# Attention and two expert layers on one core: three sets of weights for piece 0 alone become one, and the layer operands get a pool of their own

## The chip, the cores and the metric

One core of one Trainium2 chip runs the whole kernel in one launch. The metric is device time in microseconds. Three runs of the kernel before took 894.58, 894.58 and 893.46 us, median 894.58. A further execution was profiled: 893.12 us, of which the profile's span, from the first to the last instruction, is 891.3. The core's TensorE ran at a mean granted clock of 0.993 of its full speed in it. Durations below come from this one execution.

## The reference

Queries, keys and values have 4 batches, 8 heads, 576 positions and 64 channels. Attention stays inside chunks of 64 positions. Its output, as 2304 tokens x 512 channels, goes through two layers with different weights (512 x 2048 and 2048 x 512 each).

```python
scores = scale * np.matmul(q_c, k_c.transpose(0, 1, 2, 4, 3))     # chunks of 64
scores = scores - np.max(scores, axis=-1, keepdims=True)
attn = np.exp(scores)
attn = attn / (np.sum(attn, axis=-1, keepdims=True) + 1e-09)
out = np.matmul(attn, v_c)
...
h = x @ w_in1;  g = h * np.clip(h + 3.0, 0.0, 6.0) / 6.0;  x = g @ w_out1
h = x @ w_in2;  g = np.maximum(h, 0.0) + np.log1p(np.exp(-np.abs(h)));  out = g @ w_out2
```

The layers' weights arrive as 64-bit numbers and are turned into float32 on the chip.

## The kernel before

**Pieces and steps.** The 2304 tokens are cut into five pieces: piece 0 has 256 tokens, pieces 1 to 4 have 512. The 2048 hidden channels are cut into 16 sets of 128; a set of weights is one 512 x 128 block of `w_in` (half 0) and one 128 x 512 block of `w_out` (half 1). A *step* (`Step`, line 565) is one layer, one piece and one set. Every operand of a product is held as a high and a low part (fp32r), and a product takes three of the four combinations. So a step has a first product of 12 matmuls into one PSUM bank `h` (`first_product`, line 626: eight with `wh`, four with `wl`; the weights are the stationary operand and the piece's `x` is the moving one), an activation on ScalarE, VectorE and GpSimd that ends in `gh` and `gl` (`activate`, line 651), and a second product of 12 matmuls that adds into the output banks (`second_product`, line 736). In layer 1 the second product moves `gh`/`gl` over the weights, in layer 2 it moves the weights. PE gets the first product of step i+2 ahead of the second product of step i.

**Weights.** `convert` (line 281) loads the raw 64-bit words of half a set into a staging tile (512 KB a half) and makes float32 of them: two ScalarE passes (lines 299 and 302), three VectorE passes (a clamp on line 305, a shift on 311, the sign on 316) and an addition on GpSimd (line 322). The result stays in a tile of its own, `w0_0` to `w15_1`. Each time a piece begins a set, `split` (line 334) makes `wh` on ScalarE and `wl` on GpSimd or VectorE from it. The raw words of layer 1 are staged in tiles that later hold x of pieces 2 to 4 (`RAW`, line 869).

**Attention.** A `Unit` (line 372) is 512 columns of scores: two units for piece 0, four for each other piece. Its work on PE is a transpose of q and k (pieces 0 and 1 by matmul, lines 420 and 427; the others on VectorE, line 400), scores (line 466), a transpose of p (line 474) and the weighing with v (line 517). Between these stand five to eight passes on VectorE and some on ScalarE. It ends by filling the piece's `x<piece>_0` (high) and `x<piece>_1` (low). v arrives by halves of a piece in the tiles `v`, of which there are two (`load_v`, line 357).

**Order.** No order is written out by hand. All work is put into a list of jobs with their engines, costs, tiles and due times. `Schedule.run` (line 58 on) plays them through, takes for each engine the job that is due first among those that can start, and gives each a tile as soon as its former user is done. The instructions are issued in this order, so each engine, and the one DMA queue (SP), works strictly in it; an instruction that waits holds up all behind it on its engine. Due times come from a timetable of the steps (line 598): it begins at 15 us and adds each step's PE time. The units of pieces 2 to 4 are spread over the time of the piece before (line 879).

**The steps around the change.** `JOIN` is 3: with sets 0, 1 and 2 only piece 0 is worked on; from set 3 on each set serves piece 1 and then piece 0; after set 15 piece 1 does sets 0, 1 and 2 alone. Then come pieces 2, 3 and 4 of layer 1, pieces 1, 2 and 3 of layer 2, and at last pieces 4 and 0 of layer 2 side by side. In the joint stage piece 0's output takes the banks H1 and A1, so `h` has one bank, H0.

**Places in SBUF.** All tiles but the identity come from one pool, `sb`. A tile is placed when the program first uses it, behind the ones placed before: the tiles that also stage q, k and raw words (x2, x3, x4) lie low in each partition, between 17,024 and 101,184 bytes; `wh0` and `wl0` lie between 101,568 and 115,904, piece 0's x from 115,904 to 124,096, `gh` and `gl` between 134,336 and 152,768, x1 at 154,816 and 177,344, `wh1` and `wl1` between 165,056 and 175,296.

Of the kernel before, what the change touches and what calls it, by code (L numbers as in the profile page):

```python
# [8 lines left out]
F32 = mybir.dt.float32  # L9
# [161 lines left out]
def kernel(  # L171
# [20 lines left out]
    NT, DM = out.shape  # L192
    DFF = w_in1.shape[1] // 2
    P = 128
    CH = 64
    KD = DM // P
    KF = DFF // P
    NP = H // 2
# [8 lines left out]
    NPC = len(pieces)  # L207
    assert sum(tokens) == NT and tokens == [HALF] + [512] * (NPC - 1)

    const = ctx.enter_context(tc.tile_pool(name="const", bufs=1))  # L210
    sb = ctx.enter_context(tc.tile_pool(name="sb", bufs=1))
    psum = ctx.enter_context(tc.tile_pool(name="psum", bufs=1, space=bass.MemoryType.PSUM))

    BANKS = ("y0", "y1", "y2", "y3", "H0", "H1", "A0", "A1")
    bufs = dict.fromkeys(BANKS, 1)
    for f in range(KF):
        bufs[f"w{f}_0"] = bufs[f"w{f}_1"] = 1
    for x in range(NPC):
        bufs[f"x{x}_0"] = bufs[f"x{x}_1"] = 1
    bufs.update(  # L220
        wh0=2, wh1=2, wl0=2, wl1=2, gh=3, gl=3, cg=3, v=2, raw=2, qkT=1, p=3, ps=2, r=3, m=3, sm=3, rs=3,
    )
    sch = Schedule(bufs)
    ident = const.tile([P, P], F32, name="ident")

    def runs(x, a, n):

        done, at = 0, 0
        for b, s, m in pieces[x]:
            lo, hi = max(a, at), min(a + n, at + m)  # L230
            if lo < hi:
                yield lo - a, hi - lo, b, s + lo - at
            at += m
# [17 lines left out]
    def sp(n_bytes, rate):  # L251
        return {"SP": (n_bytes / rate, "dma")}
# [103 lines left out]

    def load_v(x, c, deps=(), due=1e9):

        t = Buf("v", [P, 2, DM], F32, "v")
        for g in range(2):  # L360
            for off, m, b, s in runs(x, (2 * c + g) * P, P):
                def load(e, off=off, m=m, b=b, s=s, g=g):
                    nc.sync.dma_start(
                        out=t.tile[off:off + m, g, :].rearrange("p (h d) -> p h d", h=H),
                        in_=v[b, :, s:s + m, :].rearrange("h p d -> p h d"),
                    )
                v_load.setdefault((x, 2 * c + g), []).append(sch.job(load, sp(m * DM * 4, 218e3), deps, (t,)))
            v_buf[x, 2 * c + g] = t
# [199 lines left out]
        def __init__(self, layer, x, f, first, last):  # L568
            self.layer, self.x, self.f, self.n, self.first, self.last = layer, x, f, tokens[x], first, last

    JOIN = 3
    seen = {}
    steps = []

    def add_step(layer, x, f):
        n = seen[layer, x] = seen.get((layer, x), 0) + 1
        steps.append(Step(layer, x, f, n == 1, n == KF))


    for f in range(KF):  # L580
        if f >= JOIN:
            add_step(1, 1, f)
        add_step(1, 0, f)
    for f in range(JOIN):
        add_step(1, 1, f)
    for x in range(2, NPC):
        for f in range(KF):
            add_step(1, x, f)
# [6 lines left out]
    NS = len(steps)  # L595


    t = 15.0
    for i, s in enumerate(steps):
        s.at = t  # L600
        t += 24 * (s.n / 2400.0 + 0.0133) + (2.0 if i < JOIN else 0.0) + (0.3 if s.layer == 1 else 0.0)

    def when(layer, x, nth=0):
        return [s.at for s in steps if (s.layer, s.x) == (layer, x)][nth]
# [241 lines left out]
    for u in range(2):  # L846
# [4 lines left out]
            for y, src in enumerate((q, k))  # L851
        ])
    load_v(0, 0)
    for un in units:
        un.attend()
    join = when(1, 1)
    for u in range(NP):
# [4 lines left out]
            for y, src in enumerate((q, k))  # L862
        ])
    load_v(1, 0)
    load_v(1, 1)
    for un in units[2:]:
        un.attend()

    RAW = ["x3_1", "x4_0", "x4_1", "x2_0", "x3_0", "x2_1"]
    for f in range(KF):  # L870
        tag = RAW[f] if f < len(RAW) else ("x3_1", "x4_0", "x4_1", "x3_0")[(f - len(RAW)) % 4]
        raw = Buf(tag, [P, 2, 1024], I32, "raww")
# [3 lines left out]
    before = [j for un in units for j in un.turned]  # L876
    for x in range(2, NPC):
        a, b = when(1, x - 1), when(1, x)
        us = [Unit(x, (u,), a + (b - a) * (u + 1) / NP - 2.0, ("A0", "A1"), x > 2) for u in range(NP)]
        for un in us:  # L880
            un.load(before)
            before = un.loads
        for c in range(2):
            load_v(x, c, [l for g in range(2 * c) for l in v_load[x, g]] or v_load[x - 1, 3])
        for un in us:
            un.attend()
# [17 lines left out]
    with tc.manual_schedule():  # L904
        nc.scalar.preload_act_table_set("natural_log_exp_and_others")
        for j in sch.run():
            for b in j.uses:
                if b.tile is None:
                    pool_ = psum if b.tag in BANKS else sb
                    b.tile = pool_.tile(b.shape, b.dt, tag=b.tag, name=b.name, bufs=bufs[b.tag])  # L910
            j.fn(j.engine)

# [30 lines left out]
```

## Time and profile before

| | |
|---|---|
| median of three runs | 894.58 us |
| profiled execution | 893.12 us |
| span of its profile | 891.3 us |
| PE busy | 867.3 us, 97% |
| VectorE busy | 608.8 us, 68% |
| ScalarE busy | 545.6 us, 61% |
| GpSimd busy | 456.1 us, 51% |

PE is the engine of the matmuls, DVE is VectorE, ACT ScalarE, POOL GpSimd, and SPq the queue that issues DMAs. A line L636 is line 636 of the kernel. Matmuls overlap in the pipeline, so the time of one is read from the start of one group to the start of the next, not from its duration. The releaser behind an arrow is what ended a wait.

### The profile page before, as it was taken

How to read it: one execution, taken by the hardware profiler on the slowest of the kernel's cores; microseconds unless marked ns; L12 is line 12 of the kernel's file. 1: busy time of each engine (PE TensorE's matmuls, PEld its weight loads, DVE VectorE, ACT ScalarE, POOL GpSimd, SP SyncE). 2: the span in 40 equal slices, each digit the busy share in tenths (PEclk: the TensorE clock that was granted, in tenths of full speed). 3: DMA queues.
4: the chain of work that ended last, by engine and by line, in shares of the span. 5: the costliest groups of instructions: out<-in, count | busy, mean ns of one | idle time of the engine just before them, and what ended most of it. 6: DMA issues, size and time to landing. Idle time of an engine off the chain costs nothing.

```text
span 891.3 us, 13771 instructions
## 1 busy us (share of the span) xinstructions
PE 867.3 (97%) x5112; PEld 711.5 (80%) x5112; DVE 608.8 (68%) x935; ACT 545.6 (61%) x987; POOL 456.1 (51%) x359
## 2 busy tenths in 40 slices
PE   7889999999999999999999999999999999999996
PEld 5777888887778778788888888888888888887875
DVE  5989999845345546479887655655565557778775
ACT  5855565455444545478777666666666666565654
POOL 1545556543444444469987444444444444555551
PEclk9989999999999999999999999999999999999999
DMA  9991531240112210046640000100010001000002
GB/s 275 247 236 56 158 111 56 41 79 1 25 25 48 46 28 25 24 142 192 200 151 1 1 1 0 48 1 1 0 48 1 1 0 48 1 1 1 1 1 71
DMA packets 101571, 53.33 MB, mean 60 GB/s; under 512 B 76672, under 2 KB 95104, under 8 KB 101504
## 3 DMA queue, kind: packets, MB, share of 16 engines
q1 hardware_dynamic: 101504, 52.45, 21.8%
q8 instruction: 40, 0.66, 0.3%
q14 instruction: 27, 0.22, 0.1%
HBM read 47.71 MB, written 4.72 MB: 59 GB/s over the span
## 4 chain that ended last, share of the span: by engine, by line
PE 73%; DVE 13%; ACT 5%; POOL 3%; DMA 2%; issue 2%; SPq 1%; DVEq 0%; POOLq 0%; ACTq 0%
PE y L762 33%; PE h L636 24%; PE h L643 12%; DVE r L708 3%; POOL wl L265 2%; POOL gl L265 1%; PE z L762 1%; DVE l L704 1%; DVE cg L316 1%; DVE cg L305 1%; PE ss L466 1%; DVE cg L311 1%; DVE gl L265 1%; ACT r L693 1%; DVE r L714 1%
## 5 line engine op out<-in xcount | busy, mean ns | idle before, releaser
L265 POOL TENSOR_TENSOR wl<-w,wh 128x512 fp32r<-128x512 f32 x257 | 338.4, 1318 | 321.8 <-ACT wh L260 235.8
L636 PE MATMUL h<-x,wh 128*128 128x512 f32 (+1 forms) x1280 | 295.9, 373 | 1.9 <-DVE r L674 1.7
L636 PEld LDWEIGHTS h<-x,wh 128*128 128x128 f32 x1280 | 225.9, 189 | 48.6 <-DVE r L674 2.8
L260 ACT ACTIVATE wh<-w 128x512 fp32r<-128x512 f32 x262 | 164.9, 629 | 129.2 <-PE y L762 66.0
L643 PE MATMUL h<-x,wl 128*128 128x512 f32 (+1 forms) x640 | 162.0, 374 | 0.0
L643 PEld LDWEIGHTS h<-x,wl 128*128 128x128 f32 x640 | 112.8, 189 | 22.5
L322 POOL TENSOR_TENSOR w<-w,cg 128x512 int32<-128x512 int32 x64 | 86.7, 1361 | 63.0 <-DVE cg L316 46.8
L265 DVE TENSOR_TENSOR gl<-h,gh 128x512 fp32r<-128x512 f32 x96 | 66.2, 690 | 49.2 <-ACT gh L260 48.9
L699 DVE TENSOR_SCALAR d<-r 128x512 f32<-128x512 f32 x80 | 33.0, 413 | 80.8 <-ACT r L693 80.8
L260 ACT ACTIVATE gh<-h 128x512 fp32r<-128x512 f32 x96 | 57.3, 597 | 47.7 <-DVE h L719 32.2
L708 DVE SCALAR_TENSOR_TENSOR r<-l,r 128x512 f32<-128x512 f32 x80 | 77.5, 969 | 5.1 <-DVE l L704 0.5
L762 PE MATMUL y<-wh,gh 128*128 128x512 f32 x256 | 72.9, 397 | 1.2 <-ACT gh L260 1.1
L674 DVE SCALAR_TENSOR_TENSOR h<-r,h 128x512 f32<-128x512 f32 x48 | 33.3, 694 | 58.6 <-ACT r L667 58.6
L762 PE MATMUL y<-gh,wh 128*128 128x512 f32 x256 | 72.1, 395 | 0.0
L762 PE MATMUL y<-gh,wl 128*128 128x512 f32 x256 | 71.3, 393 | 0.0
L762 PE MATMUL y<-wl,gh 128*128 128x512 f32 x256 | 70.7, 390 | 0.0
L762 PE MATMUL y<-gl,wh 128*128 128x512 f32 x256 | 70.6, 390 | 0.0
L762 PE MATMUL y<-wh,gl 128*128 128x512 f32 x256 | 70.5, 389 | 0.0
L667 ACT ACTIVATE r<-h 128x512 f32<-128x512 f32 (+1 forms) x80 | 44.2, 552 | 37.4 <-PE h L643 37.3
L260 ACT ACTIVATE gh<-r 128x512 fp32r<-128x512 f32 (+1 forms) x64 | 33.3, 521 | 52.7 <-DVE r L719 24.2
L704 DVE TENSOR_TENSOR l<-l,d 128x512 f32<-128x512 f32 x80 | 54.2, 678 | 14.9 <-ACT l L696 13.1
L762 PEld LDWEIGHTS y<-wh,gh 128*128 128x128 f32 x256 | 47.3, 188 | 16.6 <-ACT gh L260 5.7
(77 smaller groups left out, 1142.5 us busy)
## 6 DMA issues: line engine op xcount, KB each, us to landing
raww<-in_moe_w_in_dram SPq DMA_DIRECT2D x32, 512.0 KB, 4.1
raww<-in_moe_w_out_dram SPq DMA_DIRECT2D x32, 512.0 KB, 4.7
v<-in_v_dram SPq DMA_DIRECT2D x16, 256.0 KB, 5.8
out_dram<-o SPq DMA_DIRECT2D x16, 256.0 KB, 2.0
raw<-in_q_dram SPq DMA_DIRECT2D x32, 64.0 KB, 2.5
raw<-in_k_dram SPq DMA_DIRECT2D x32, 64.0 KB, 2.5
nat<-in_q_dram SPq DMA_DIRECT2D x4, 256.0 KB, 6.5
nat<-in_k_dram SPq DMA_DIRECT2D x4, 256.0 KB, 6.7
```

The source lines that it names most:

```text
L260: nc.scalar.activation(out=out, in_=in_, func=AF.Copy)
L265: (nc.vector if e == "DVE" else nc.gpsimd).tensor_tensor(out=out, in0=in0, in1=in1, op=ALU.subtract)
L305: nc.vector.tensor_scalar(out=t.tile, in0=t.tile, scalar1=LEAST, scalar2=MOST, op0=ALU.max, op1=ALU.min)
L322: nc.gpsimd.tensor_tensor(out=w.tile, in0=w.tile, in1=g.tile.bitcast(I32), op=ALU.add)
L636: nc.tensor.matmul(out=h.tile[:, :n], lhsT=hi.tile[:, kk * P:(kk + 1) * P], rhs=x.tile[:, kk, :], start=(kk == 0 and m == 0), stop=False,)
L643: nc.tensor.matmul(out=h.tile[:, :n], lhsT=lo.tile[:, kk * P:(kk + 1) * P], rhs=xh.tile[:, kk, :], start=False, stop=(kk == KD - 1),)
L667: nc.scalar.activation(out=of(r), in_=of(h), func=AF.Relu, bias=3.0)
L674: lambda e: nc.vector.scalar_tensor_tensor(out=of(g), in0=of(r), scalar=6.0, in1=of(h), op0=ALU.min, op1=ALU.mult), dve(n), (j,), (h, r), due,
L699: lambda e: nc.vector.tensor_scalar(out=of(d), in0=of(r), scalar1=1.0, scalar2=1.0, op0=ALU.add, op1=ALU.subtract), dve2(n), (u,), (r, d),
L704: lambda e: nc.vector.tensor_tensor(out=of(l), in0=of(l), in1=of(d), op=ALU.subtract),
L708: lambda e: nc.vector.scalar_tensor_tensor(out=of(r), in0=of(l), scalar=0.0, in1=of(r), op0=ALU.min, op1=ALU.add), dve(n, not stays), (j,) ...
L762: nc.tensor.matmul(out=bank.tile[:, col:col + width], lhsT=lhs, rhs=rhs, start=(s.first and m == 0 and opens), stop=(s.last and m == 2 and ...
```

## The change

Three things. `JOIN` becomes 1, with another order: piece 0's set 0, then piece 1's set 0, then for sets 1 to 14 piece 1 before piece 0, and for set 15 piece 0 before piece 1; no set is left for piece 1 alone. The timetable begins at 28 us, and the four units of piece 2 are due in the second half of the joint stage (2/6 of it later). The second v tile of piece 1 is `x4_1`, and the first raw words go through the tiles in another order. And a pool `streamed`, opened behind `sb`, holds `wh`, `wl`, `gh`, `gl` and all x.

```diff
     sb = ctx.enter_context(tc.tile_pool(name="sb", bufs=1))
+    streamed = ctx.enter_context(tc.tile_pool(name="streamed", bufs=1))
...
+    STREAMED = {"wh0", "wl0", "wh1", "wl1", "gh", "gl"} | {f"x{x}_{part}" for x in range(NPC) for part in range(2)}
...
-        t = Buf("v", [P, 2, DM], F32, "v")
+        t = Buf("x4_1" if (x, c) == (1, 1) else "v", [P, 2, DM], F32, "v")
...
-    JOIN = 3
+    JOIN = 1
...
     for f in range(KF):
-        if f >= JOIN:
-            add_step(1, 1, f)
-        add_step(1, 0, f)
-    for f in range(JOIN):
-        add_step(1, 1, f)
+        for x in (1, 0) if JOIN <= f < KF - 1 else (0, 1):
+            add_step(1, x, f)
...
-    t = 15.0
+    t = 28.0
...
-    RAW = ["x3_1", "x4_0", "x4_1", "x2_0", "x3_0", "x2_1"]
+    RAW = ["x3_1", "x4_0", "x2_0", "x2_1", "x3_0", "x4_1"]
...
-        us = [Unit(x, (u,), a + (b - a) * (u + 1) / NP - 2.0, ("A0", "A1"), x > 2) for u in range(NP)]
+
+        late = 2 if x == 2 else 0
+        us = [
+            Unit(x, (u,), a + (b - a) * (u + 1 + late) / (NP + late) - 2.0, ("A0", "A1"), x > 2) for u in range(NP)
+        ]
...
-                    pool_ = psum if b.tag in BANKS else sb
+                    pool_ = psum if b.tag in BANKS else streamed if b.tag in STREAMED else sb
```

## Rows read from the trace of the kernel before

**Rows 1.** The page, busy time, share of the span and instructions of each engine.
```profile
PE 867.3 (97%) x5112; PEld 711.5 (80%) x5112; DVE 608.8 (68%) x935; ACT 545.6 (61%) x987; POOL 456.1 (51%) x359
```
**Rows 2.** Table by stage: length, busy us (instructions) by engine, clock, DMA share, GB/s.
```profile
44.76:69.61 24.85, 20.09 (x130) 17.06 (x128) 22.00 (x38) 13.51 (x27) 10.90 (x9) 0.86 0.88 213
69.61:174.57 104.96, 104.11 (x764) 89.72 (x764) 101.50 (x139) 59.85 (x116) 61.54 (x46) 1.00 0.31 86
...
387.85:476.28 88.43, 88.43 (x385) 72.03 (x384) 76.75 (x120) 70.74 (x126) 77.95 (x62) 1.00 0.52 157
493.30:564.02 70.72, 70.72 (x313) 58.56 (x312) 41.23 (x65) 46.70 (x78) 33.73 (x26) 1.00 0.00 1
564.02:652.66 88.64, 88.64 (x385) 71.95 (x384) 53.10 (x84) 58.79 (x97) 41.34 (x32) 1.00 0.03 13
751.01:784.39 33.38, 33.38 (x169) 28.25 (x168) 25.07 (x35) 19.72 (x40) 19.02 (x16) 1.00 0.09 32
784.39:870.73 86.34, 86.14 (x421) 69.91 (x420) 66.06 (x91) 50.42 (x101) 46.97 (x40) 1.00 0.00 1
```
**Rows 3.** What PE waited for, 0 to 100 us: total, times, longest.
```profile
PE z L762 <- ACT wh L260: 3.8, 1, 3.8
...
PE h L636 <- DVE r L674: 1.7, 2, 0.9
```
**Rows 4.** The same view, 100 to 891 us.
```profile
PE y L762 <- ACT gh L260: 1.1, 2, 0.9
```
**Rows 5.** PE in order of time: start, us, instruction, idle before.
```profile
44.76 2.02 PE L636 MATMUL h<-x,wh 128*128 128x512 f32 x8
...
51.44 1.22 PE L762 MATMUL z<-gh,wh 128*128 128x256 f32 x4 [3.76 <-ACT wh L260]
...
65.64 1.11 PE L636 MATMUL h<-x,wh 128*128 128x256 f32 x8
...
67.07 0.64 PE L762 MATMUL z<-gh,wh 128*128 128x256 f32 x4
...
69.61 0.73 PE L636 MATMUL h<-x,wh 128*128 128x512 f32 x2 [0.94 <-DVE r L674]
```
**Rows 6.** The same view, one step of pieces 1 and 2 in layer 2.
```profile
498.74 1.98 PE L636 MATMUL h<-x,wh 128*128 128x512 f32 x8
500.55 1.07 PE L643 MATMUL h<-x,wl 128*128 128x512 f32 x4
501.46 1.07 PE L762 MATMUL y<-wh,gh 128*128 128x512 f32 x4
...
602.80 2.03 PE L636 MATMUL h<-x,wh 128*128 128x512 f32 x8
604.67 1.09 PE L643 MATMUL h<-x,wl 128*128 128x512 f32 x4
605.60 1.08 PE L762 MATMUL y<-wh,gh 128*128 128x512 f32 x4
```
**Rows 7.** DVE by line, 9.3 to 45.8 us: count, busy us, mean ns, idle before.
```profile
L311 DVE TENSOR_SCALAR cg<-cg 128x512 int32<-128x512 int32 x6 | 3.5, 580 | 0.1
L316 DVE SCALAR_TENSOR_TENSOR cg<-raww,cg 128x512 int32<-128x512 int32 x5 | 3.4, 683 | 0.0
L305 DVE TENSOR_SCALAR cg<-cg 128x512 f32<-128x512 f32 x6 | 2.8, 459 | 0.3 <-ACT cg L299 0.3
...
L674 DVE SCALAR_TENSOR_TENSOR r<-r,h 128x256 f32<-128x256 f32 x3 | 1.2, 411 | 0.0
```
**Rows 8.** ACT in order of time, the wait behind which the split stood.
```profile
48.83 0.66 ACT L302 ACTIVATE w<-raww 128x512 int32<-128x512 uint32 x1 [3.85 <-DMA raww<-in_moe_w_in_dram]
```
**Rows 9.** The DMA queue in order of time.
```profile
43.30 0.42 SPq L291 DMA_DIRECT2D raww<-in_moe_w_in_dram  x1
```
**Rows 10.** PE in order of time, piece 2's last unit: scores, and past its weighing.
```profile
169.37 1.15 PE L466 MATMUL ss<-qkT 64*64 64x64 f32 x32
...
187.57 1.19 PE L643 MATMUL h<-x,wl 128*128 128x512 f32 x4
```

## The prediction

> **What bounds the kernel now.** I read the page's busy shares first, then a table by stage, then what TensorE (PE) waited for, then the order of PE's work in the first 70 us, and last the spacing of its matmuls inside a step. The shares say PE: 867.3 of 891.3 us [rows 1]. The waits say where it is not PE: before 100 us it waited 3.8 us once for a weight split and 1.7 us for VectorE (DVE) [rows 3], and after 100 us 1.1 us in all [rows 4]. So time can come only from the head, up to about 70 us, or from PE's own work running faster.
>
> *The head.* Piece 0 does its first three products alone; piece 1 enters at 44.76 us; the next second product comes at 51.44 after the 3.76 us wait; from 69.61 on PE hardly stops [rows 5]. [...] I need one number for the head: when PE would have started if it had done nothing but products, without a gap. By 69.61 it had done five first products of piece 0 (1.44 us each at full clock: the row at 65.64 and its wl products end 1.43 later at 67.07), four second products of piece 0 (1.44 each), two first and one second product of piece 1 (2.72 each): 9 x 1.44 + 3 x 2.72 = 21.1 us. One score product of piece 2 (1.1 us) was done too. So the effective start is 69.6 - 21.1 - 1.1 = 47.4 us.
>
> *The products.* The table by stage splits the dense part by piece. In layer 2, piece 1 takes 70.72 us for 13 steps (312 of the matmuls counted), 5.440 each; piece 2 takes 88.64 for 16, 5.540 each; in layer 1 piece 4 takes 88.43 for 16, 5.527 [rows 2]. It is the same work on the same shapes, and PE is busy 100% in all three. Inside a step the first product shows it: from the start of the eight wh matmuls to the start of the wl matmuls it takes 500.55 - 498.74 = 1.81 us for piece 1 and 604.67 - 602.80 = 1.87 for piece 2, and the four wl matmuls 0.91 and 0.93 [rows 6]. That is some 6.5 ns a matmul. The weights and the elementwise work are the same; what differs is where the moving operand lies. Tiles of a pool lie in the order of their first use, and adding up sizes gives their start in a partition: x2 and x3 at 17,024 to 53,888 bytes, x4 at 70,272 and 92,992, piece 0 at 115,904, gh at 134,336, x1 at 154,816 and 177,344. The slow moving operands are the low ones; gh and x1, above 134,336, run at 0.227 us a matmul.
>
> **The change, part by part.**
>
> *Layer operands in a pool of their own.* It removes no instruction. Pools are stacked in the order opened: const ends at 17,024, what stays in `sb` is 109,120 bytes, so `streamed` (102,400 bytes) begins at 126,144 and every x, gh, gl, wh, wl lies above. If the row reading holds, pieces 2 to 4 run as piece 1 does: in layer 1 pieces 2 and 3 (32 steps x 0.100; their windows hold attention too, so I take layer 2's difference) and piece 4 (16 x 0.087), in layer 2 pieces 2 and 3 (32 x 0.100): 3.2 + 1.4 + 3.2 = 7.8 us. The last stage, piece 4 beside piece 0, is different: four pairs take 33.38 us, 8.35 each, but the ten from 784.39 take 86.34, 8.63 each [rows 2]: there the elementwise chain sets the pace, and a faster product only waits longer. I count the other six pairs, 6 x 0.087 = 0.5. Sum 8.3 us. Upper bound, all sixteen: 9.2. Lower bound by place: the first tile of the pool, half of x2, lies at 126,144 to 134,336, below the lowest address shown fast with 512 columns; if it stays slow, 8 of 12 first-product matmuls in 32 steps do: 32 x 0.100 x 2/3 = 2.1 lost, 6.2 left. Lower bound by cause: 0, if place is not it.
>
> [...]
>
> *Piece 1 from the first set of weights on.* The matmuls are the same in number. Gone are re-splits of three sets at the end of the joint stage (six wh, six wl, on ScalarE and GpSimd, beside a PE that has no wait there), so nothing. What moves is the head. What sets when piece 1 is ready is DVE, which works almost without a gap until piece 1's fills are done (0.3 us is all the idle time before the groups shown [rows 7]); the first product of piece 1 starts at 44.76 [rows 5]. Up to there DVE runs 6 clamps (0.459 us), 6 shifts (0.580), 5 signs (0.683) of the weight conversion and 3 products of piece 0's activation (0.41) [rows 7]. Before piece 1 is needed the new order asks for three conversions (both halves of set 0, the first half of set 1) and one activation: out of the way go 3 x 0.459 + 3 x 0.580 + 2 x 0.683 + 2 x 0.41 = 5.3 us. Piece 1 starts at 44.76 - 5.3 = 39.5. The work put behind it comes due at once: five conversions (8.6 us) within the next 11 us, and the normal activations; here I expect waits.
>
> *Waits after the start.* Before, the 24.85 us from 44.76 to 69.61 held 2 x 2.72 + 2 x 1.44 + 3 x 1.44 + 2.72 + 1.1 = 16.5 us of work; 8.4 were lost to waits and the low clock. One cause was the ACT queue: its next instruction, a conversion of a set far ahead, waited 3.85 us for weights issued only at 43.30 behind piece 2's q and k loads [rows 8, 9], and the split that PE needed stood behind it. The change puts piece 2's units later (2/6 of the stage), so their loads come due later; a like mistake can still happen. Loss after the new start: at best the 1.7 us that DVE cost [rows 3], at worst 8.4 again; I take half of it, 4.2. New effective start: 39.5 - 1.44 (piece 0's first product, done before) + 4.2 = 42.3, against 47.4: 5.1 us gained. Bounds: 7.6 with 1.7 lost; 0.9 with 8.4; if piece 1 is no earlier than now, -0.2, and with 8.4 lost -4.4.
>
> *Other tiles for v and raw words.* The second v tile of piece 1 goes to x4_1, raw sets 2, 3 and 5 change tile. No copy or load more; a v load need not wait for piece 0's v. Set 2 now waits for x2_0, which piece 0's q leaves before 10 us; set 5 waits for piece 1's last weighing and is used 30 us later. I take 0; bounds -0.5 and +0.5, one 0.5 us issue slot either way.
>
> *Sum.* 8.3 + 5.1 = 13.4 us. The profiled execution took 893.12 us: 879.7. The median of the timed runs is 894.58, 1.46 above it: 881.2, say 881.
>
> **The rivals.**
> A, *place is nothing*: only the head gains. For it: the x2 to x4 steps differ from x1's in neighbours too. Against: the slow-down sits on the first product alone, and the step is as long in layer 1 (5.527) as in layer 2 (5.540), whose elementwise work differs [rows 2]. 894.6 - 5.1 = 889.5.
> [...]
> C, *piece 2 late*, slower than before: today three steps of piece 1 alone (3 x 5.44 us from 174.57 on), with no weights left to convert, precede piece 2 and let DVE finish its attention; they go, and its four units are pushed into the second half of the joint stage. The last unit, scores to weighing, takes 187.57 - 169.37 = 18.2 us [rows 10]. If it starts when piece 2 is due, PE waits 18.2: 894.6 - 13.4 + 18.2 = 899.4. It turns slower above a wait of 13.4. Against: the last unit's due time, 2 us before piece 2, is unchanged.
>
> **How the numbers follow.** Forecast 0.57, B 0.18, A 0.13, C 0.08, the rest 0.04. The range takes the forecast's bounds (9.2 + 7.6 gives 877.8; 3 us below for waits I do not see), A and B, and the upper end 891 is the placement gain with the worst head (890.7): 875 to 891. About 0.2% (1.8 us) is what a measurement tells from no change. Faster: forecast, B, A and half the rest: 0.88. Same 0.04, slower 0.08.
>
> **What would show it.** Place: steps of pieces 2 to 4 in layer 2 at 5.44 us; at 5.54, A. Half of x2: piece 2 alone near 5.50. Head: piece 1's first product near 40 us, PE dense well before 69 us; a first product at 45 or later refutes the DVE count. C: a PE gap where piece 2 begins in layer 1. The prediction is wrong if both groups of steps stay as they are or the joint stage ends later than 191 us.

## The result, and the profile after

The changed kernel takes 879.08 us (median of 4 runs, 877.49 to 880.32), the one before 894.02 beside it (4 runs, 893.23 to 894.58): ratio 0.9833, 95% interval 0.9814 to 0.9851. The forecast was 881. The profiled execution took 879.37 us with a span of 877.6, 13.7 less than before. Cut at the first products of piece 2 (layer 1), of layer 2 and of its last stage, the spans give:

| stretch | before, us | after, us | change | forecast |
|---|---|---|---|---|
| start to piece 2 of layer 1 | 191.35 | 184.75 | -6.6 | -5.1 |
| layer 1, pieces 2 to 4 | 284.93 | 282.20 | -2.7 | -4.6 |
| layer 2, piece 1 | 87.74 | 87.93 | +0.2 | 0 |
| layer 2, pieces 2 and 3 | 177.28 | 174.08 | -3.2 | -3.2 |
| last stage and end | 149.97 | 148.62 | -1.35 | -0.5 |

The page's first part and the table by stage of the changed kernel answer to [rows 1, 2]; the columns are the same.

```profile
PE 857.7 (98%) x5112; PEld 709.6 (81%) x5112; DVE 603.7 (69%) x934; ACT 540.6 (62%) x986; POOL 443.3 (51%) x349
```
```profile
35.52:68.80 33.28, 29.93 (x162) 24.08 (x157) 28.84 (x45) 21.48 (x43) 17.99 (x13) 1.00 0.66 162
68.80:174.79 105.99, 104.64 (x771) 89.73 (x770) 99.73 (x148) 62.79 (x123) 58.15 (x41) 1.00 0.37 100
...
379.91:466.95 87.04, 87.04 (x385) 72.07 (x384) 75.62 (x119) 68.56 (x125) 76.86 (x62) 1.00 0.52 159
484.17:554.89 70.72, 70.72 (x314) 58.56 (x312) 41.44 (x65) 46.69 (x78) 33.67 (x26) 1.00 0.00 1
554.89:641.93 87.04, 87.04 (x386) 72.07 (x384) 53.09 (x84) 57.81 (x97) 41.44 (x32) 1.00 0.04 13
738.59:771.63 33.04, 33.04 (x170) 28.27 (x168) 25.33 (x35) 20.34 (x41) 18.90 (x16) 1.00 0.09 33
```

All three product windows now run at 5.440 us a step: 70.72 / 13, and 87.04 / 16 where 88.64 and 88.43 stood. In the head the clock column reads 1.00 where it read 0.86; that is this one execution: the other three had mean granted clocks of 0.994 to 0.996, against 0.999 here, and took 877.49 to 880.32 us, so the clock is not what the gain hangs on. PE in order of time shows piece 1 starting at 35.52 instead of 44.76, and one step of piece 2 in layer 2 with 1.81 us for the eight wh matmuls, as piece 1 had [rows 5, 6]:

```profile
31.73 1.22 PE L636 MATMUL h<-x,wh 128*128 128x256 f32 x8
...
35.52 1.43 PE L636 MATMUL h<-x,wh 128*128 128x512 f32 x5
...
43.13 0.71 PE L762 MATMUL z<-gh,wh 128*128 128x256 f32 x4 [0.83 <-DVE r L674]
...
68.80 2.00 PE L636 MATMUL h<-x,wh 128*128 128x512 f32 x8
...
191.18 2.14 PE L636 MATMUL h<-x,wh 128*128 128x512 f32 x8 [0.83 <-DVE x L803]
...
554.89 1.98 PE L636 MATMUL h<-x,wh 128*128 128x512 f32 x8
556.70 1.07 PE L643 MATMUL h<-x,wl 128*128 128x512 f32 x4
```

The waits of PE up to 100 us, without those for the first loads, answer to [rows 3]: the single 3.8 us wait is gone, the short ones on VectorE remain.

```profile
PE h L636 <- DVE r L674: 2.1, 4, 0.6
PE oo L520 <- DVE p L490: 1.1, 1, 1.1
PE y L762 <- ACT wh L263: 0.9, 1, 0.9
```

VectorE by line up to 37.5 us answers to [rows 7]: two conversions where six had begun (L308 is the clamp, L314 the shift, L319 the sign), and the normalization of p (L481).

```profile
L481 DVE TENSOR_TENSOR p<-p,rs 128x512 f32<-128x512 f32 x6 | 4.2, 720 | 0.1
...
L319 DVE SCALAR_TENSOR_TENSOR cg<-raww,cg 128x512 int32<-128x512 int32 x2 | 1.4, 692 | 0.1
...
L314 DVE TENSOR_SCALAR cg<-cg 128x512 int32<-128x512 int32 x2 | 0.9, 426 | 0.0
L308 DVE TENSOR_SCALAR cg<-cg 128x512 f32<-128x512 f32 x2 | 0.8, 420 | 0.0
...
L674 DVE SCALAR_TENSOR_TENSOR r<-r,h 128x256 f32<-128x256 f32 x1 | 0.4, 417 | 0.0
```

### The profile page after: what moved, and what is told of

The parts are those of the page before. It is cut to its first block, busy times and chain, and to the rows that moved or that the text cites. A ratio compares the mean times of both kernels' runs of the same rounds, so it can differ in the third digit from the quotient of the medians.

```text
span 877.6 us, 13743 instructions
## 1 busy us (share of the span) xinstructions
PE 857.7 (98%) x5112; PEld 709.6 (81%) x5112; DVE 603.7 (69%) x934; ACT 540.6 (62%) x986; POOL 443.3 (51%) x349
## 5 line engine op out<-in xcount | busy, mean ns | idle before, releaser
L268 POOL TENSOR_TENSOR wl<-w,wh 128x512 fp32r<-128x512 f32 x249 | 328.7, 1322 | 310.4 <-ACT wh L263 235.6
L636 PE MATMUL h<-x,wh 128*128 128x512 f32 (+1 forms) x1280 | 290.7, 369 | 3.5 <-DVE r L674 2.1
L636 PEld LDWEIGHTS h<-x,wh 128*128 128x128 f32 x1280 | 225.3, 188 | 47.4 <-DVE r L674 3.4
L263 ACT ACTIVATE wh<-w 128x512 fp32r<-128x512 f32 x256 | 160.5, 628 | 113.7 <-PE y L762 63.1
L643 PE MATMUL h<-x,wl 128*128 128x512 f32 (+1 forms) x640 | 159.1, 370 | 0.0
L325 POOL TENSOR_TENSOR w<-w,cg 128x512 int32<-128x512 int32 x64 | 86.2, 1352 | 74.6 <-DVE cg L319 39.5
```

The lines of the kernel that those rows point to most:

```text
L263: nc.scalar.activation(out=out, in_=in_, func=AF.Copy)
L268: (nc.vector if e == "DVE" else nc.gpsimd).tensor_tensor(out=out, in0=in0, in1=in1, op=ALU.subtract)
L325: nc.gpsimd.tensor_tensor(out=w.tile, in0=w.tile, in1=g.tile.bitcast(I32), op=ALU.add)
L636: nc.tensor.matmul(out=h.tile[:, :n], lhsT=hi.tile[:, kk * P:(kk + 1) * P], rhs=x.tile[:, kk, :], start=(kk == 0 and m == 0), stop=False,)
L643: nc.tensor.matmul(out=h.tile[:, :n], lhsT=lo.tile[:, kk * P:(kk + 1) * P], rhs=xh.tile[:, kk, :], start=False, stop=(kk == KD - 1),)
```

## The experiments

Spans are of one profiled execution each; intervals come from timed runs beside the kernel before.

**The two halves alone.** `pool_only` is the kernel before with the second pool; `order_only` the changed one without it.

```diff
-                    pool_ = psum if b.tag in BANKS else sb
+                    pool_ = psum if b.tag in BANKS else streamed if b.tag in STREAMED else sb
```


> The kernel before with the layer operands in the second pool, order and timetable as before. Theory (a moving operand low in the partition slows each matmul by 6.5 ns): pieces 2 to 4 step in 5.44 us, about 8.5 us saved, 885.5 us. Rival 1 (what counts is the start address modulo 128 bytes; the slow tiles were at 0, the fast ones at 64, and the new pool starts at 64): the same 885.5. Rival 2 (place is nothing, the order does all): 894, steps still 5.54.

> The changed kernel with all tiles in one pool again; x2 and half of x3 start at 0 modulo 128 bytes, x4 and the other half of x3 at 64, all of them below 93,000 bytes. Theory: layer-2 steps of pieces 2, 3 and 4 at 5.54 us, total 879.1 + 8.5 = 887.6. Rival 1: piece 2 at 5.54, piece 3 in between, piece 4 at 5.44. Rival 2: about 879, with 5.44 everywhere.

`pool_only`: 887.25 us, ratio 0.9924 (0.9900 to 0.9947), span 884.3. Its head is as long as before (piece 2 at 191.36 against 191.35); from there on it gains 7.0 us. `order_only`: 887.12 us, ratio 0.9913 (0.9898 to 0.9928), span 885.7. Piece 2 starts at 185.35, 6.0 us earlier, and nothing is gained behind. So the two effects are separate and about equal, and rivals A (only the head gains) and B (the head gains nothing) are both out. Against rival 1, `order_only` has piece 4 at 64 modulo 128 bytes, and it steps in 5.53.

**High, low, or the start's last bits.** Shown is the pad of `high_shift64`; `low_shift64` also opens `streamed` ahead of `sb`.

```diff
-    ident = const.tile([P, P], F32, name="ident")
+    ident = const.tile([P, P + 16], F32, name="ident")[:, :P]
```


> The changed kernel with 64 bytes more ahead of the pools, so that every layer operand starts at 0 modulo 128 bytes, still above 126,000. Theory: nothing changes, 5.44 us a step, 879 us. Rival 1: every step is slow, first and second products, 5.54 us or more, 879 + 128 x 0.1 = 892 or more.

> The changed kernel with the operand pool below the other one: x from 17,088 to 99,008, gh and gl at 99,008 to 111,296, wh1 and wl1 up to 119,488, all at 64 modulo 128 bytes. Theory: first products of all 512-token pieces slow, piece 1 too (128 steps x 0.1 = 12.8 us): 892, and up to 905 if the second products' moving operands lie low enough as well. Rival 1: as fast as the changed kernel, 879.

`high_shift64` 879.02 us, `low_shift64` 880.54: both fast, 87.04 us for the 16 steps of piece 2 in layer 2. The first rules out rival 1: there every operand starts at 0 modulo 128. The second overturns the prediction's reading: there x lies at 17,088 to 99,008 bytes and runs at full speed. Piece 2 in `low_shift64`, by the table by stage:

```profile
555.88:642.92 87.04, 87.04 (x386) 72.09 (x384) 53.12 (x84) 57.80 (x97) 41.72 (x32) 1.00 0.03 13
```

**Crossing a border.** `x_high_only` leaves only x in the pool; `x_low_only` does the same with that pool opened first.

```diff
-    STREAMED = {"wh0", "wl0", "wh1", "wl1", "gh", "gl"} | {f"x{x}_{part}" for x in range(NPC) for part in range(2)}
+    STREAMED = {f"x{x}_{part}" for x in range(NPC) for part in range(2)}
```


> The changed kernel with x alone in the second pool (from 154,816); wh0 and wl0 now at 56,512 to 64,710, gh at 79,040 to 85,184, gl at 95,424 to 101,568, wh1 and wl1 at 101,568 to 109,760. New theory: a matmul is slow (6.5 ns) when its moving operand lies below a border, somewhere between 82,624 and 101,568, and its weights above it. Then layer-1 second products are slow (gh moving low, wh1 high; some 0.05 to 0.1 us a step, 5.50 to 5.54) and gl shows by its three buffers where the border is; first products (x high, wh0 low) and layer-2 second products (wh1 moving high, gh low) stay at 0.227 us. Rival S (either crossing is slow): first products slow in both layers and layer-2 second products too, 5.60 us a step or more. Rival C (a moving operand is slow among tiles that other engines work on): second products slow in both layers, first products fast.

> The changed kernel with x alone in the pool and that pool below (x of all pieces at 17,024 to 90,752), everything else above 90,752, the elementwise tiles p, l, cg, r at 111,424 to 150,720, wh0 and wl0 at 130,240 to 138,432. New theory: every first product of a 512-token piece is slow, piece 1 too: layer-2 steps of pieces 1, 2 and 3 at 5.54 us, 879 + 128 x 0.1 = 892. Rival C: no other engine works among x, so all steps at 5.44 us and 879.

`x_high_only`: 878.07 us, span 876.3, every product fast (87.04 us for the 16 steps of piece 2 in layer 2, and a span below the changed kernel's 877.6), gh below and wh1 above the supposed border included: that theory falls too. `x_low_only`: 888.87 us, span 887.1, and every piece of 512 tokens slow: in layer 2 piece 2 takes 88.64 us for 16 steps, and piece 1 is slow too, 72.02 us for the 13 steps of this row, 5.54 each:

```profile
488.38:560.40 72.02, 72.02 (x313) 58.46 (x312) 41.51 (x65) 47.37 (x78) 33.60 (x26) 1.00 0.00 1
```

The time is some 3 us below the 892 expected: piece 2 starts at 184.87, as in the changed kernel, so the slower steps of piece 1 in the joint stage cost nothing that shows. Rival C is out: no other engine works among these x tiles. What the slow and the fast cases differ in is the start of x less the start of its weights. In `x_low_only` and in pieces 2 and 3 before it is -576 modulo 2048; in all the cases so far that were fast it is 0. The 576 bytes are the nine tiles m, sm and rs of 64 bytes, the only tiles behind x whose size is no multiple of 2048.

**Moving 576 bytes.** `small_first` is the kernel before, one pool, with these nine tiles ahead of it. `gaps_a` is the changed kernel with small gaps ahead of x1 to x4.

```diff
+    small = ctx.enter_context(tc.tile_pool(name="small", bufs=1))
     sb = ctx.enter_context(tc.tile_pool(name="sb", bufs=1))
...
-                    pool_ = psum if b.tag in BANKS else sb
+                    pool_ = psum if b.tag in BANKS else small if b.tag in ("m", "sm", "rs") else sb
```


> The kernel before, one pool as before, with only the nine 64-byte tiles m, sm and rs moved ahead of it: x2, x3 and x4_0 move up by 576 bytes, x4_1 by 384, nothing else moves. All tiles then have the same start modulo 2048 (1216). Theory 3 (a matmul with 512 columns is slow when the starts of its moving operand and its weights differ modulo some power of two, and high or low does not matter): pieces 2 to 4 step in 5.44 us, 887 us as with the second pool. Rival (the border between low and high): x stays low and the weights high, so 5.54 and 894 as before.

> The changed kernel with x1, x2, x3 and x4 in pools of their own above the weights, 64, 128, 256 and 512 bytes off the weights' start modulo 2048. Theory 3: at least some of pieces 1 to 4 are slow in both layers again, up to 5.54 us a step, though everything lies above 126,000; if the modulus is 128, piece 1 alone; if 256, pieces 1 and 2; if 512, pieces 1 to 3. Rival (absolute start modulo 256 decides, slow at 64 and 128): pieces 2 and 4 fast or slow by their own starts, 1344 and 1728 modulo 2048, that is 64 and 192 modulo 256: piece 2 slow, pieces 1, 3 (1280 and 1472: 0 and 192) and 4 fast.

`small_first`: 889.37 us, ratio 0.9944 (0.9923 to 0.9964). Its 16 steps of piece 2 in layer 2, by the table by stage:

```profile
563.75:650.79 87.04, 87.04 (x385) 72.11 (x384) 53.10 (x84) 57.87 (x97) 41.40 (x32) 1.00 0.03 13
```

x2 went from 17,024 to 17,600 and is fast. From piece 2 of layer 1 to the end it takes 887.45 - 194.49 = 693.0 us, `pool_only` 884.29 - 191.36 = 692.9, the kernel before 699.9: the move does all that the pool does. Its head was 3.1 us longer than before (piece 2 at 194.49), with the same order of instructions on every engine. The mean granted clock of this execution was 0.989, and 1.00 from 195 us on; the kernel before had a mean of 0.993, `pool_only` 0.992. Over their spans these means are 9.8, 6.2 and 7.1 us short of full clock, so by estimate the lower clock cost this execution 2.7 to 3.5 us more than those two, about these 3.1. Why the clock was lower is open. `gaps_a`, 885.67 us, by the same table: piece 1 (64 bytes off, 13 steps), piece 2 (128 off, 16 steps), piece 3 (256 off, 16 steps), all in layer 2.

```profile
487.98:559.89 71.91, 71.91 (x313) 58.60 (x312) 41.50 (x65) 47.45 (x78) 33.80 (x26) 1.00 0.00 1
559.89:648.32 88.43, 88.43 (x385) 72.09 (x384) 53.04 (x84) 58.56 (x97) 41.39 (x32) 1.00 0.04 13
648.32:735.36 87.04, 87.04 (x385) 72.08 (x384) 53.10 (x84) 57.82 (x97) 41.41 (x32) 1.00 0.04 13
```

That is 5.53, 5.53 and 5.44 us a step, and piece 4 (512 off, in layer 1) takes 5.44: 64 and 128 bytes are slow, 256 and 512 are not, as Theory 3 has it for a modulus of 256. The rival by absolute start would have piece 1 fast (its start, 1280 modulo 2048, is that of the weights and x in `high_shift64`); it is slow.

**The head.** Each is the changed kernel with one edit taken back: `t15` the timetable (28 to 15), `late0` the later units of piece 2, `old_v` the v tile, `old_tiles` the v tile and the staging tiles.

```diff
-        t = Buf("x4_1" if (x, c) == (1, 1) else "v", [P, 2, DM], F32, "v")
+        t = Buf("v", [P, 2, DM], F32, "v")
```


> The changed kernel with the second v tile of piece 1 back in v and the raw words in the old tiles. Theory for the head (piece 1 is early because VectorE converts fewer weights before it): piece 1 still starts within 1 us of 35.5 us, piece 2 within 1 us of 184.8. Rival (the free v tile and the staging tiles make it early): piece 1 starts after 38 us.

> The changed kernel with the timetable beginning at 15 us again. Theory (the order of the steps keeps conversions away from VectorE): piece 1 starts within 1.5 us of 35.5. Rival (it is the later timetable that lets attention go first): conversions move up again and piece 1 starts at 38 us or later, piece 2 at 187 or later.

> The changed kernel with the second v tile of piece 1 back in v; the raw words stay in the new tiles. Theory (that v load can only go once piece 0 is weighed, and then stands on the DMA queue behind piece 2's q and k): PE waits some 10 us for v, piece 1 starts near 50 us, piece 2 near 197, 890 us. Rival (the raw words' tiles did it): piece 1 starts within 2 us of 35.5, 879 us.

> The changed kernel with piece 2's units spread over the whole joint stage as before. Theory (the later due times keep piece 2's loads and attention out of the start): piece 1 starts as early, but the stretch up to piece 2's first product is longer by 1 to 4 us, 880 to 883. Rival (they change nothing): within 1 us, 878 to 880.

| run | us | span | piece 1 starts | piece 2 starts |
|---|---|---|---|---|
| after | 879.37 (profiled) | 877.6 | 35.5 | 184.8 |
| `t15` | 880.07 | 878.3 | 35.7 | 185.5 |
| `late0` | 881.12 | 879.3 | 34.8 | 185.9 |
| `old_tiles` | 891.65 | 889.6 | 50.8 | 197.9 |
| `old_v` | 893.96 | 891.8 | 51.8 | 200.0 |

`t15` and `late0` are 0.7 and 1.7 us longer in span, of one execution each. Both came out as their theories had it, but the changed kernel's own four runs spread over 2.8 us: too little to call either edit needed. The v tile is another matter. `old_tiles` refutes its theory, and `old_v` shows that the v tile alone does it. What PE waited for in `old_v` up to 100 us, and its DMA queue:

```profile
PE oo L520 <- DMA v<-in_v_dram: 12.2, 2, 11.6
```
```profile
29.83 7.51 SPq L395 DMA_DIRECT2D raw<-in_q_dram  x4
37.39 4.25 SPq L395 DMA_DIRECT2D raw<-in_k_dram  x4
41.74 1.06 SPq L366 DMA_DIRECT2D v<-in_v_dram  x2
```

The second v tile of piece 1 has to wait for piece 0's, and by then it stands behind eight loads of piece 2 on the queue that take 11.9 us. PE waits 11.6 us, and its mean granted clock over the run is 0.986, against 0.999 in the changed kernel's profiled execution: behind the wait 64 matmuls of the weighing take 2.24 us (49.53 to 51.77), where in the kernel before 32 took 0.62 us at a clock of 1.00 (19.00 to 19.62). In the changed kernel all four v loads of piece 1 are issued together:

```profile
14.30 6.07 SPq L366 DMA_DIRECT2D v<-in_v_dram  x4
```

## Why the prediction was right and where it was wrong

*What bounds the kernel, and where time can come from:* right. The head and the product rate gave nearly all of it. That the total came so close, 13.7 us of span for 13.4, is in part luck: the head gave 1.5 us more than forecast and the last stage 0.85 more, layer 1 gave 1.9 less. (Forecast, B, A and half the rest add up to 0.90, not 0.88.)

*Layer operands in a pool of their own:* the size was right, the cause wrong. The step that failed is "the slow moving operands are the low ones". They were those whose start differed from their weights' start by 64, 128 or 192 bytes modulo 256 (5.53 to 5.54 us a step, against 5.44 at 0, 256 and 512); the pool removes this because all its tiles are multiples of 2048 bytes. The rows could not separate the two, since before every low x was also 576 or 384 bytes off. A list of starts modulo small powers of two would have brought up this rival. By [rows 6] the first product holds 0.08 of the 0.100 us that a slow step is longer (2.80 against 2.72); the other 0.02 lies in the second product behind it, whose own operands start alike. Term by term: layer 2, pieces 2 and 3, -3.2 as forecast; layer 1, piece 4, 88.43 - 87.04 = 1.39 for 1.4; layer 1, pieces 2 and 3, only 1.3 for 3.2. In `pool_only` all of layer 1's pieces 2 to 4 gain 3.9, so about 2.5 for these two: steps that hold attention gained 0.08 each, not 0.100. In the changed kernel 0.83 more went into a wait at 191.18, where piece 2's second step stands behind x values of piece 0 (line 803). The bound "half of x2 stays slow" did not come about.

*The lower bound by cause, 0, if place is not it:* place is it. 576 bytes changed the 16 steps of piece 2 in layer 2 from 88.64 us to 87.04 with the same instructions (`small_first`). By what means the place slows these matmuls no run here shows.

*Piece 1 from the first set on:* right in direction, too small. I had piece 1 at 39.5; it came at 35.5. VectorE ran two conversions ahead of it, not three: conversion and activation took 10.9 us before [rows 7] and 3.5 after, 7.4 less where 5.3 was forecast. And six normalizations of p took 4.2 us where five had taken 5.5. Three of those five began while GpSimd was at an addition (line 322) and took 1.17 to 1.76 us; the other two, and all but one after, took 0.68 to 0.69. In the kernel before, in order of time:

```profile
14.69 1.27 POOL L322 TENSOR_TENSOR w<-w,cg 128x512 int32<-128x512 int32 x1 [13.38 <-ACT qkT L260]
...
15.28 1.24 DVE L478 TENSOR_TENSOR p<-p,rs 128x512 f32<-128x512 f32 x1
...
16.66 0.69 DVE L478 TENSOR_TENSOR p<-p,rs 128x512 f32<-128x512 f32 x1
```

The normalization at 15.28 began inside the addition and took 1.24 us, the one at 16.66 began after it and took 0.69; why it takes longer beside the addition no run here shows. The prediction's list of PE's waits before 100 us left out the one on these normalizations, 2.9 us of it at once, up to 38.33 us; after, PE waits 0.4 us there.

```profile
PE tt L474 <- DVE p L478: 3.6, 2, 2.9
```

*Waits after the start:* 4.2 forecast, 5.6 measured (35.52 to 68.80 is 33.28 us for 27.7 of products). Of the 8.4 us lost before, the low clock is a part: it was 0.50 from 51 to 54 us and 0.51 from 54 to 57; after, it is 1.00 from 35.52 to 68.80. The effective start, worked out as in the prediction, is 68.80 - 7 x 1.44 - 7 x 2.72 = 39.7, against 42.3 forecast and 47.4 before. Of the 7.7 us so gained 1.1 are lost in the joint stage up to piece 2.

*Other tiles for v and raw words, taken at 0:* wrong, and the largest miss. The order without the v tile ends at a span of 891.8, as late as the kernel before, though it has the pool, which alone ended at 884.3: without the v tile the new order costs 7.5 us. In the order as it was PE did not wait for that load; the prediction did not follow it into the new order, where it stands behind piece 2's loads. The new order is worth its 6 us only because the v tile makes the load early. The v tile with the old order was not run.

*The last stage:* -1.35 for -0.5. In the other runs in which piece 4 steps in 5.44 us this stretch took between 148.5 and 149.6, and 149.4 to 150.0 in the three in which piece 4 is slow, so I do not put the difference down to anything.

*Rival C:* piece 2 was not late; the 0.83 us wait at its second step is all there is.

## What to carry to other kernels

Where the same matmul runs at two speeds in one kernel, list the starts of its operands modulo 64 to 2048 bytes before believing in regions: here a few 64-byte tiles between the large ones cost 7 us (699.9 against 693.0 from piece 2 of layer 1 to the end), and placing them first, in `small_first`, took it back. When work is moved forward, follow each of its loads in the new order to the tile it must wait for and to its place on the queue. An edit that looks like bookkeeping may be what makes the rest work.

## What the runs showed of the hardware

In these runs a matmul of 512 fp32r columns started every 0.227 us when its moving operand and its weights began at the same address modulo 256 bytes (differences of 0, 256 and 512), and on average every 0.230 us at a difference of 64, every 0.233 at 128 and 192 (a first product of 2.76 and 2.79 us in `gaps_a` and 2.80 in the kernel before, against 2.72); high or low and across did not matter (87.04 us for 16 steps in `high_shift64`, `low_shift64` and `x_high_only`, all at a difference of 0). For 256 columns, in the one step shown, it went the other way: in `x_low_only`, at a difference of 192, piece 0's first product takes 754.31 - 752.90 = 1.41 us in the last stage, against 1.43 and 1.44 in two steps of the kernel before (764.88 to 766.31, 756.53 to 757.97).

```profile
752.90 1.10 PE L636 MATMUL h<-x,wh 128*128 128x256 f32 x8
...
754.31 0.62 PE L762 MATMUL z<-wh,gh 128*128 128x512 f32 x2
```

Differences that are no multiple of 64, and other widths, were not tried. In every run all weights and `gh`, `gl` started alike modulo 256, so whether a matmul's own weights count or those loaded for the next was not separated; why the difference counts stays open.
